# Long convolution with a gated output: the transposed signal's stores on two other queues, two pairs of it loaded early, and whole-partition reads before the last stage

## The chip, the cores and the metric

The kernel runs on one core of a Trainium2 chip. The metric is device time in microseconds from start to end of one execution. Five engines take part: TensorE (PE, its weight loads PEld), VectorE (DVE), ScalarE (ACT), GpSimd (POOL) and SyncE (SP). Each runs its own list of instructions in order and waits for the others by semaphores. A DMA is issued by one engine (it stands in that engine's list and waits its turn there) and is then carried by 16 DMA engines, which all the queues share. Everything is f32.

## The reference

```python
# x, v: [4, 12800, 128]; pos_emb: [12800, 64]
h = np.maximum(pos_emb @ w1, 0) @ w2 * np.exp(-0.01 * pos)[:, None]
y = causal convolution of (x * v) with h along the sequence, per channel (by FFT)
z = x * y
gate = sigmoid(sum over k < 5 of conv_w[k] * z shifted down by 4 - k)   # per channel
out = (gate * (z @ w_val)) @ w_out
```

## The kernel before

The convolution is a transform over a split index: 12800 positions are J = 2 halves of N1 = 100 by N2 = 64. Two arrays in DRAM stand between three stages: `a_u`, the signal after the transform over N1, 105 MB in both directions together, and `c_y`, the product with the filter's spectrum, transformed back over N2, about as much. Instructions are put in each engine's list in the order in which the code issues them.

**Stage 1 (lines L232 to L388, up to some 356 us)** has 64 iterations. For each, `fetch` (L306) loads 1 MB of x and v into one of five `ld` tiles, seven iterations ahead, on SP's queue. `product` (L312, DVE) multiplies them; `mirrored` (every second iteration) makes sums and differences `eo` on DVE (L321) and POOL (L322), in two buffers by turns; `spectra` does 12 matmuls into `fp` (L334, PE) and two evictions into `st` (L336, ACT; four buffers). `store` writes the first 100 partitions of `st` to `a_u`, on SP's queue and one iteration late: each iteration calls `store(*last)`, and `_Split` (L118) makes two DMAs of it, 96 rows and 4 rows. In between, a generator `fil` puts the work on the filter (`gp`, `ap`, `fk`, `ag`) into the lists of PE, DVE and ACT, a portion each iteration. In iteration 62 the table of weights (`in_tab_w`) and 24 of the 32 slices of pair 0 of `a_u` are loaded.

**Stage 2 (L391 to L520, to some 755 us)** goes over 50 pairs p of frequencies. `load_pair` reads 1 MB of `a_u` for a pair (L227; L213 where `load_a` reads a part of one), two pairs ahead. `filter_pair` (L404) makes the pair's filter, evicted into `h_sb` (L409); `spectrum` (L419) transforms the signal into `z_ps`; `times` (L425, DVE) multiplies both into `va`, `vb`, `vc`, `vd`; POOL adds them (L504 to L506); `inverse` transforms back into `c_ps` (L435), ACT copies that into `c_sb` (L442; two tiles, each with both halves j) and stores 512 KB to `c_y` from ACT's queue (L443). From p = 34 on, `load_k` (L202) reads rows of `c_y` that are complete into `ag` blocks, for the first FIRST = 3 steps of stage 3.

**Stage 3 (L530 to L725)** has 32 steps s of R = 4 rows. `load_rows` reads the step's 2 MB of `c_y` into two `ag` blocks, by `_Split` in eight DMAs of 96 or 4 partitions, and `load_x` a tile `xr` (L545), on SP. `y_sum` (L596, PE, with the table `inv`, over 100 partitions) makes `sd`, `y_copy` (L603, ACT) copies it to `sd_sb`, `y_trans` (L610) transposes it, `y_join` (L621 on DVE, L623 on POOL) multiplies by x into `ext`; then come the five taps (L638, DVE), the sigmoid (L644), the two products (`v_ps` L649, `o_ps` L659) and the store of the result from ACT's queue (L671). The tiles of this stage lie in pools opened when stage 2's are closed.

Of the kernel before, what the change touches and what calls it, by code (L numbers as in the profile page):

```python
# [28 lines left out]
R = 4  # L29
WARM = 4  # L30
NC1 = N1 // 2 + 1


def _tables():
# [87 lines left out]
def tile_longconv_gate(  # L122
# [28 lines left out]
    c_y = dram.tile([J, N1, 2 * N2, B, D], F32, name="c_y")  # L151
# [3 lines left out]
    inv = const.tile([N1, 2, N2], F32, name="inv")  # L155
# [19 lines left out]
    nc.scalar.dma_start(out=inv, in_=t_inv)  # L175
# [16 lines left out]
    blocks = [ag.rearrange("p k j e -> p (k j e)")[:N1, i * CR:(i + 1) * CR] for i in range(N1 * J * FO // CR)]  # L192
# [3 lines left out]
    def block(s, c):  # L196
        return blocks[(2 * s + c) % len(blocks)]

    def load_k(s, c, k0, k1):
        j, g = y_order[s]  # L200
        n0 = c * N2 + g * R
        nc.sync.dma_start(  # L202
            out=block(s, c)[k0:k1], in_=c_y[j, k0:k1, n0:n0 + R].rearrange("k p b d -> k (p b d)"))
# [3 lines left out]
    weights, loaded, NL = [], {}, 24  # L207
# [24 lines left out]
    with tc.tile_pool(name="p1", bufs=1) as p1, tc.tile_pool(name="ps1", bufs=1, space=PSUM) as ps1:  # L232
# [106 lines left out]
        def store(q, s, st):  # L339
            sync_s.dma_start(  # L340
                out=a_u[:, s, q].rearrange("k e j b d -> k (e j b d)"),
                in_=st[:N1].rearrange("k e j b d -> k (e j b d)"))

        fetched, us, eos, last = {}, {}, {}, None
        with tc.manual_schedule():
# [15 lines left out]
            for n in range(N2):  # L361
# [26 lines left out]
            store(*last)  # L388


    with tc.tile_pool(name="p2", bufs=1) as p2, tc.tile_pool(name="ps2", bufs=1, space=PSUM) as ps2:  # L391
# [3 lines left out]
        def bank():  # L395
            return ps2.tile([128, BD], F32, name="z_ps", bufs=4)

        def filter_pair(p):

            h_ps = ps2.tile([128, J, BD], F32, name="c_ps", bufs=2)[:, :, 0:2 * D].rearrange("p j (c d) -> p j c d", c=2)  # L400
# [28 lines left out]
        def inverse(p, j, terms):  # L429
            wk = loaded[p][1]  # L430
            c_ps = ps2.tile([128, 2, BD], F32, name="c_ps", bufs=2)
# [6 lines left out]
            if j == 0:  # L438
                c_sb = p2.tile([128, 2, J, B, D], F32, name="c_sb", bufs=2)
                outs[p] = c_sb  # L440
            c_sb = outs[p]
            nc.scalar.copy(out=c_sb[:, :, j].rearrange("p h b d -> p h (b d)"), in_=c_ps)  # L442
            nc.scalar.dma_start(  # L443
                out=c_y[j, 2 * p:2 * p + 2].rearrange("h p b d -> p h (b d)"),
                in_=c_sb[:, :, j].rearrange("p h b d -> p h (b d)"))

        outs = {}
# [11 lines left out]
        with tc.manual_schedule():  # L459
            for p in range(-1, NP + 1):  # L460
                now, nxt, old = 0 <= p < NP, p + 1 < NP, 0 <= p - 1
                if p < 0:
                    load_a(loaded[0][0], 0, NL, N2 // 2)
                for q in range(AHEAD + 1) if p < 0 else (p + AHEAD,):
                    if q < NP and q not in loaded:
                        loaded[q] = load_pair(q)
                if p in early:
                    load_k(*early.pop(p))
# [26 lines left out]
                if now:  # L495
                    vc = p2.tile([128, 2, B, D], F32, name="vc", bufs=3)
                    vd = p2.tile([128, 2, B, D], F32, name="vd", bufs=2)
                    times(vc, z1[0], h[:, 0, 0:2], 2)
# [5 lines left out]
                    nc.gpsimd.tensor_tensor(va[:, 0:2], va[:, 0:2], vb[:, 0:2], op=ALU.add)  # L504
                    nc.gpsimd.tensor_tensor(vcf, vcf, vdf, op=ALU.add)  # L505
# [4 lines left out]
                if old:  # L510
                    if p < NP:
                        inverse(p - 1, 0, ((0, oa[:, 0]), (1, oa[:, 1])))
                    if p == NP - 1:
                        inverse(p, 0, ((0, va[:, 0]), (1, va[:, 1])))
                        for c in range(2):
                            load_k(0, c, 96, N1)
                    inverse(p - 1, 1, ((0, oa[:, 2]), (1, oa[:, 3, 0:PB]), (0, oc[:, 0]), (1, oc[:, 1])))
            for s in range(1, FIRST):
                for c in range(2):
                    load_k(s, c, 80, N1)  # L520
# [9 lines left out]
    with tc.tile_pool(name="p3", bufs=1) as p3, tc.tile_pool(name="ps3", bufs=1, space=PSUM) as ps3:  # L530
# [8 lines left out]
        def load_x(s):  # L539
# [4 lines left out]
            xr = p3.tile([D, R * ROW], F32, name="xr", bufs=2)  # L544
# [47 lines left out]
        def y_sum(s, r):  # L592
            ct, _ = loads3[s]
            sd = ps3.tile([128, B * D], F32, name="sd", bufs=2)
            for c in range(2):
                nc.tensor.matmul(  # L596
                    out=sd[c * N2:(c + 1) * N2], lhsT=inv[:, c], rhs=ct[c][:, r * B * D:(r + 1) * B * D],
# [3 lines left out]
        def y_copy(s, r):  # L601
            t = p3.tile([128, B, D], F32, name="sd_sb", bufs=3)
# [3 lines left out]
        def y_trans(s, r):  # L606
            t = sds.pop((s, r))
            tp = ps3.tile([D, B, 128], F32, name="tp3", bufs=2)
            for b in range(B):
                nc.tensor.transpose(out=tp[:, b], in_=t[:, b], identity=ident)  # L610
            dif = p3.tile([D, B, NC1], F32, name="dif", bufs=3)
# [3 lines left out]
        def y_join(s, r):  # L615
# [3 lines left out]
            yr = p3.tile([D, B, N1], F32, name="yr", bufs=2)  # L619
# [59 lines left out]
        with tc.manual_schedule():  # L679
# [93 lines left out]
```

## Time and profile before

| | |
|---|---|
| median of 3 runs | 1147.57 us (1146.57 to 1148.95) |
| the profiled execution | 1147.54 us |
| its span, from the first to the last instruction | 1145.8 us |
| granted TensorE clock, mean | 0.970 |
| busy: PE, DVE, POOL, ACT | 1041.9, 969.1, 781.2, 615.9 us |
| moved by DMA | 344.60 MB, 301 GB/s over the span |

The page of the profile gives each engine's busy time over the whole span. The stages have different limits, so busy times in stretches of a stage, the waits in it and the chain of the work that ended last say more. A rate in GB/s counts what the DMA engines moved in a stretch, and the DMA share is the mean part of it in which they were busy.

### The profile page before, as it was taken

The numbers are of one execution on the slowest core, as the hardware profiler recorded it, in microseconds if no ns is written. First come the engines' busy times: TensorE is split into PE (matmuls) and PEld (weight loads), VectorE is DVE, ScalarE is ACT, GpSimd is POOL, SyncE is SP. The second block draws the span as 40 slices with busy tenths as digits, with TensorE's granted clock in tenths as the row PEclk, the third lists the DMA queues.
The fourth block names the chain that finished last, engine by engine and source line by source line (L and its number), as shares of the span: only waits on it lengthen the run. The fifth ranks groups of instructions, "written<-read, shape, count | busy, mean of one in ns | idle before, by whom it ended". The sixth has DMA issues, their size and how long they took to land.

```text
span 1145.8 us, 17528 instructions
## 1 busy us (share of the span) xinstructions
PE 1041.9 (91%) x6208; PEld 490.5 (43%) x6208; DVE 969.1 (85%) x1150; ACT 615.9 (54%) x1003; POOL 781.2 (68%) x393
## 2 busy tenths in 40 slices
PE   4899898777874999999999999988999999999996
PEld 2455554433431344444444444433444444444442
DVE  5675545799844999999999999819999999999997
ACT  1366555766751344444344434337777767767674
POOL 3353432233312888988898888928999899999981
PEclk9999998999995899999999999989999999999999
DMA  9999999999987688888888999575999999999952
GB/s 361 367 413 406 366 361 358 345 358 345 361 265 291 223 307 310 299 309 304 307 285 284 364 352 329 192 212 165 297 283 297 277 296 291 293 292 287 291 174 115
DMA packets 93176, 344.60 MB, mean 301 GB/s; under 512 B 9806, under 2 KB 19706, under 8 KB 77898
## 3 DMA queue, kind: packets, MB, share of 16 engines
q1 hardware_dynamic: 58824, 263.74, 70.2%
q10 hardware_dynamic: 34266, 79.74, 18.1%
q8 instruction: 51, 0.84, 0.3%
q14 instruction: 35, 0.29, 0.1%
HBM read 212.37 MB, written 131.07 MB: 300 GB/s over the span
## 4 chain that ended last, share of the span: by engine, by line
PE 66%; DMA 24%; DVE 5%; ACT 3%; issue 1%; SPq 0%; ACTq 0%; DVEq 0%
PE c_ps L435 22%; DMA a_u<-st 13%; PE sd L596 10%; PE z_ps L419 9%; DMA ld<-in_xv_dram 8%; PE o_ps L659 7%; PE v_ps L649 6%; PE tp L610 5%; PE fp L334 3%; PE c_ps L404 2%; DMA ld<-in_pos_dram 2%; DVE gt L638 1%; DVE fk L284 1%; ACT st L336 1%; PE gp L292 1%
## 5 line engine op out<-in xcount | busy, mean ns | idle before, releaser
L623 POOL TENSOR_TENSOR ext<-yr,xr 128x400 f32<-128x400 f32 x120 | 304.6, 2540 | 34.3 <-DVE yr L621 31.3
L322 POOL TENSOR_TENSOR eo<-eo 128x512 f32<-128x512 f32 x62 | 120.0, 1954 | 204.6 <-DVE eo L321 204.6
L638 DVE SCALAR_TENSOR_TENSOR gt<-ext,cw,gt 128x1600 f32<-128x1600 f32 x128 | 241.1, 1884 | 2.4 <-ACT gt L635 2.4
L334 PE MATMUL fp<-eo,fold 64*128 64x512 f32 x768 | 196.3, 646 | 51.1 <-ACT st L336 36.5
L442 ACT COPY c_sb<-c_ps 128x1024 f32<-128x1024 f32 x100 | 101.3, 1013 | 203.2 <-PE c_ps L435 193.9
L336 ACT COPY st<-fp 128x1024 f32<-128x1024 f32 x128 | 124.5, 1015 | 130.0 <-DMA a_u<-st 71.4
L435 PE MATMUL c_ps<-va,ld 64*128 64x512 f32 (+1 forms) x800 | 165.3, 552 | 0.0
L425 DVE TENSOR_TENSOR va<-z_ps,h_sb 128x2048 f32<-128x2048 f32 x50 | 114.4, 2287 | 36.9 <-DMA ld<-a_u 30.0
L504 POOL TENSOR_TENSOR va<-va,vb 128x1024 f32<-128x1024 f32 x50 | 118.4, 2367 | 39.9 <-DVE vb L425 39.9
L419 PE MATMUL z_ps<-ld 64*64 64x512 f32 x800 | 122.7, 620 | 17.2 <-DMA ld<-a_u 15.7
L334 PEld LDWEIGHTS fp<-eo,fold 64*128 64x128 f32 x768 | 75.0, 198 | 133.6 <-issue 76.4
L596 PE MATMUL sd<-ag,inv 100*64 100x512 f32 x512 | 129.1, 622 | 0.2 <-DMA ag<-c_y 0.2
L435 PEld LDWEIGHTS c_ps<-va,ld 64*128 64x128 f32 x800 | 73.7, 188 | 112.8 <-issue 110.0
L659 PE MATMUL o_ps<-gd,wout 128*128 128x400 f32 x256 | 111.5, 517 | 10.7 <-DVE gd L654 8.7
L506 POOL TENSOR_TENSOR va<-va,vb 128x1024 f32<-128x1024 f32 x50 | 118.2, 2363 | 0.0
L425 DVE TENSOR_TENSOR vb<-z_ps,h_sb 128x2048 f32<-128x2048 f32 x50 | 114.0, 2281 | 0.0
L603 ACT COPY sd_sb<-sd 128x512 f32<-128x512 f32 x128 | 76.6, 599 | 64.2 <-PE sd L596 55.8
L649 PE MATMUL v_ps<-ext,wval 128*128 128x400 f32 x256 | 107.2, 500 | 0.0
L610 PEld LDWEIGHTS tp<-ident,sd_sb 128*128 128x128 f32 x512 | 59.4, 143 | 81.4 <-PE sd L596 49.6
L435 PE MATMUL c_ps<-vc,ld 64*128 64x512 f32 x400 | 94.2, 589 | 0.0
L505 POOL TENSOR_TENSOR vc<-vc,vd 128x768 f32<-128x768 f32 x50 | 91.1, 1822 | 2.2 <-issue 0.3
L610 PE MATMUL tp<-ident,sd_sb 128*128 128x128 f32 x512 | 81.3, 284 | 7.0 <-ACT sd_sb L603 5.7
(84 smaller groups left out, 1452.7 us busy)
## 6 DMA issues: line engine op xcount, KB each, us to landing
ld<-in_xv_dram SPq DMA_DIRECT2D x64, 1024.0 KB
c_y<-c_sb ACTq DMA_DIRECT2D x100, 512.0 KB
ld<-a_u SPq DMA_DIRECT2D x49, 1024.0 KB
a_u<-st SPq DMA_DIRECT2D x64, 768.0 KB
ag<-c_y SPq DMA_DIRECT2D x116, 384.0 KB
xr<-in_xt_dram SPq DMA_DIRECT2D x31, 800.0 KB
out_dram<-o_sb ACTq DMA_DIRECT2D x31, 800.0 KB
ld<-in_tab_w_dram SPq DMA_DIRECT2D x12, 768.0 KB
```

Source lines behind the costliest of these rows:

```text
L322: eng.tensor_tensor(eo[:, s, :, 0], eo[:, s, :, 0], eo[:, s, :, 1], op=ALU.subtract)
L334: nc.tensor.matmul(out=fp[:, h], lhsT=fold[r, w], rhs=eo[r, o, :, l], start=i == 0, stop=i == len(terms) - 1)
L336: nc.scalar.copy(out=st[:, o].rearrange("k j (h b) d -> k h j (b d)", h=2), in_=fp)
L419: nc.tensor.matmul(out=zs[c][half[h]], lhsT=wk[half[c], 0, half[h]], rhs=a2[half[c], h, j], start=True, stop=True)
L425: nc.vector.tensor_tensor(out, z.rearrange("p (b d) -> p b d", d=D).unsqueeze(1).to_broadcast([128, n, B, D]), h_sb.unsqueeze(2).to_broadc ...
L435: nc.tensor.matmul(out=c_ps[:, h, 0:n], lhsT=wk[half[h], 1 + c], rhs=vt[half[h]].rearrange("p b d -> p (b d)"), start=(i == 0), stop=(i == ...
L596: nc.tensor.matmul(out=sd[c * N2:(c + 1) * N2], lhsT=inv[:, c], rhs=ct[c][:, r * B * D:(r + 1) * B * D], start=True, stop=True)
L610: nc.tensor.transpose(out=tp[:, b], in_=t[:, b], identity=ident)
L623: nc.gpsimd.tensor_tensor(e[:, r0 + r], yr, xr, op=ALU.mult)
L638: nc.vector.scalar_tensor_tensor(gt, rows(t, k), cw[:, k:k + 1], gt, op0=ALU.mult, op1=ALU.add)
L649: nc.tensor.matmul(out=v_ps, lhsT=wval, rhs=rows(t)[:, r * ROW:(r + 1) * ROW], start=True, stop=True)
L659: nc.tensor.matmul(out=o_ps, lhsT=wout, rhs=gd, start=True, stop=True)
```

## The change

Stage 1 stores each iteration's `st` in that iteration: 96 rows from ACT's queue, behind the two evictions that fill it, and 4 rows from POOL's. SP's queue keeps the loads alone. In iteration 60 the weights and 28 of the 32 slices of pairs 0 and 1 are loaded; the other 4 of each follow when stage 1's stores are issued.

In stage 2 each `c_sb` eviction has a tile of its own (five buffers). Of the last pair's three additions two go to DVE. All last rows of `c_y` for steps 0 to 2 are asked for within pair 49, none behind it. The table `inv` is loaded at p = 4 into the tile of the `fold` table, which is no longer needed then, and not at the start.

In stage 3 the tiles of the chain from `sd` to `yr` and `xr` are in pools of their own, which are opened first, in place of tiles that share room with stage 2's. `c_y` is laid out with both halves j below one another, 200 rows, and a block is read by one DMA of 128 rows, 1 MB: rows 0 to 127 for j = 0, rows 72 to 199 for j = 1. `inv` has zeros for the 28 rows that do not belong to j, and `y_sum` runs over 128 partitions. Two warming matmuls instead of four stand ahead of the stage.

```diff
-        def store(q, s, st):
-            sync_s.dma_start(
-                out=a_u[:, s, q].rearrange("k e j b d -> k (e j b d)"), in_=st[:N1]...)
+            for eng, r in ((nc.scalar, slice(0, 96)), (nc.gpsimd, slice(96, N1))):
+                eng.dma_start(
+                    out=a_u[r, s, q].rearrange("k e j b d -> k (e j b d)"), in_=st[r]...)
...
-                if n == N2 - 2:
-                    loaded[0] = load_pair(0, NL)              # NL = 24
-                if last:
-                    store(*last)
-                last = q, s, st
+                if n == N2 - 4:
+                    for p in range(2):
+                        loaded[p] = load_pair(p, NL)          # NL = 28
+                store(q, s, st)
...
-            store(*last)
+            for p in range(2):
+                load_a(loaded[p][0], p, NL, N2 // 2)
...
-            if j == 0:
-                c_sb = p2.tile([128, 2, J, B, D], F32, name="c_sb", bufs=2)
+            c_sb = p2.tile([128, 2, BD], F32, name="c_sb", bufs=5)
...
+                    if not nxt:
+                        nc.vector.tensor_tensor(va[:, 0:2], va[:, 0:2], vb[:, 0:2], op=ALU.add)
...
-                rows_ = c_y[j].rearrange("k p b d -> k p (b d)")
-                for h in range(0, R, R // 2):
-                    sync_s.dma_start(
-                        out=t[:, h * B * D:(h + R // 2) * B * D],
-                        in_=rows_[:, n0 + h:n0 + h + R // 2].rearrange("k p e -> k (p e)"))
+                nc.sync.dma_start(
+                    out=t, in_=c_y[j * EDGE:j * EDGE + 128, n0:n0 + R].rearrange("k p b d -> k (p b d)"))
...
+            k = slice(0, N1 if s < NG else 128)
...
-                    out=sd[c * N2:(c + 1) * N2], lhsT=inv[:, c], rhs=ct[c][:, r * B * D:(r + 1) * B * D],
+                    out=sd[c * N2:(c + 1) * N2], lhsT=inv[k, s // NG, c], rhs=ct[c][k, r * B * D:(r + 1) * B * D],
...
-    with tc.tile_pool(name="p3", bufs=1) as p3, tc.tile_pool(name="ps3", bufs=1, space=PSUM) as ps3:
+    with tc.tile_pool(name="y3", bufs=1) as y3, tc.tile_pool(name="psy", bufs=1, space=PSUM) as psy, \
+            tc.tile_pool(name="p3", bufs=1) as p3, tc.tile_pool(name="ps3", bufs=1, space=PSUM) as ps3:
```

Line numbers after the change are some two higher (L306 is L308, L334 is L336, L336 is L338). SP's list at the end of stage 1, behind the last load of x and v, before (`ld<-in_tab_w` is the table of weights, `ld<-a_u` a part of pair 0, which in the list below of the change is a part of pair 0 or 1; the stores are those of the last four iterations):

```order
L118 DMA a_u<-st 96x2048
L118 DMA a_u<-st 4x2048
L221 DMA ld<-in_tab_w_dram 128x4x384
L213 DMA ld<-a_u 48x2x1024 x2
L118 DMA a_u<-st 96x2048
L118 DMA a_u<-st 4x2048
L118 DMA a_u<-st 96x2048
L118 DMA a_u<-st 4x2048
L213 DMA ld<-a_u 16x2x1024
L118 DMA a_u<-st 96x2048
L118 DMA a_u<-st 4x2048
L213 DMA ld<-a_u 16x2x1024
```

The same place in SP's list now:

```order
L308 DMA ld<-in_xv_dram 128x2048 x50
L223 DMA ld<-in_tab_w_dram 128x4x384
L215 DMA ld<-a_u 56x2x1024 x4
L215 DMA ld<-a_u 8x2x1024 x4
L229 DMA ld<-a_u 128x2x1024 x2
```

The stores have left SP's list; the large parts of two pairs and then the small ones stand behind the last load. ACT's list in the last iterations of stage 1, where the last portion of the filter's work ends, before:

```order
L281 ACTIVATE fk<-dft,tw 128x128 x4
L295 COPY ag<-gp 128x512
L336 COPY st<-fp 128x2x2x256 x2
L295 COPY ag<-gp 128x512
L336 COPY st<-fp 128x2x2x256 x12
```

and now, with a store behind each iteration's two evictions and that iteration's portion of the filter:

```order
L283 ACTIVATE fk<-dft,tw 128x128 x4
L297 COPY ag<-gp 128x512
L343 DMA a_u<-st 96x2048
L338 COPY st<-fp 128x2x2x256 x2
L297 COPY ag<-gp 128x512
L343 DMA a_u<-st 96x2048
L338 COPY st<-fp 128x2x2x256 x2
L343 DMA a_u<-st 96x2048
```

POOL's list there had the subtractions alone; now each pair of subtractions (for the next q) has the 4-row stores of two iterations behind it:

```order
L324 TENSOR_TENSOR eo_109<-eo_109 128x2x256 x2
L343 DMA a_u<-st 4x2048 x2
L324 TENSOR_TENSOR eo_108<-eo_108 128x2x256 x2
L343 DMA a_u<-st 4x2048 x6
L506 TENSOR_TENSOR va<-va,vb 128x1024
```

A subtraction now stands behind stores that wait for evictions. SP's list from the last reads of `c_y` in stage 2 to the first full block of stage 3, before:

```order
L202 DMA ag<-c_y 16x2048 x2
L202 DMA ag<-c_y 4x2048 x2
L202 DMA ag<-c_y 20x2048 x4
L545 DMA xr<-in_xt_dram 128x1600 x2
L118 DMA ag<-c_y 96x1024
L118 DMA ag<-c_y 4x1024
```

and now:

```order
L204 DMA ag<-c_y 16x2048 x6
L204 DMA ag<-c_y 4x2048 x6
L549 DMA xr<-in_xt_dram 128x1600 x2
L561 DMA ag<-c_y 128x2048 x2
L549 DMA xr<-in_xt_dram 128x1600
```

Eight DMAs of a step have become two.

More of the change, by code (lines that the diff above doesn't have):

```diff
@@ L149, in tile_longconv_gate @@
     a_u = dram.tile([N1, 2, N2 // 2, 2, J, B, D], F32, name="a_u")
-    c_y = dram.tile([J, N1, 2 * N2, B, D], F32, name="c_y")
+    c_y = dram.tile([J * N1, 2 * N2, B, D], F32, name="c_y")
     fwd = const.tile([N1, 3, N1], F32, name="fwd")
     fold = const.tile([128, 3, 128], F32, name="fold")
-    inv = const.tile([N1, 2, N2], F32, name="inv")
+    inv = fold[:, 0:2].rearrange("p j (c n) -> p j c n", c=2)
     win = const.tile([N1, J, N2], F32, name="win")
@@ L202, in load_k @@
         nc.sync.dma_start(
-            out=block(s, c)[k0:k1], in_=c_y[j, k0:k1, n0:n0 + R].rearrange("k p b d -> k (p b d)"))
+            out=block(s, c)[k0:k1], in_=c_y[j * N1 + k0:j * N1 + k1, n0:n0 + R].rearrange("k p b d -> k (p b d)"))
     NP, PG = N1 // 2, KG // 2
-    weights, loaded, NL = [], {}, 24
+    weights, loaded, NL = [], {}, 28
     def load_a(a2, p, n0, n1):
@@ L395, in bank @@
         def bank():
-            return ps2.tile([128, BD], F32, name="z_ps", bufs=4)
+            return psz.tile([128, BD], F32, name="z_ps", bufs=4)
         def filter_pair(p):
-            h_ps = ps2.tile([128, J, BD], F32, name="c_ps", bufs=2)[:, :, 0:2 * D].rearrange("p j (c d) -> p j c d", c=2)
+            h_ps = psc.tile([128, J, BD], F32, name="c_ps", bufs=2)[:, :, 0:2 * D].rearrange("p j (c d) -> p j c d", c=2)
             for c in range(2):
@@ L430, in inverse @@
             wk = loaded[p][1]
-            c_ps = ps2.tile([128, 2, BD], F32, name="c_ps", bufs=2)
+            c_ps = psc.tile([128, 2, BD], F32, name="c_ps", bufs=2)
             for i, (c, vt) in enumerate(terms):
@@ L437, in inverse @@
                         start=(i == 0), stop=(i == len(terms) - 1))
-            if j == 0:
-                c_sb = p2.tile([128, 2, J, B, D], F32, name="c_sb", bufs=2)
[L440 to L447, printed above, removed]
+            c_sb = p2.tile([128, 2, BD], F32, name="c_sb", bufs=5)
+            nc.scalar.copy(out=c_sb, in_=c_ps)
+            nc.scalar.dma_start(out=c_y[j * N1 + 2 * p:j * N1 + 2 * p + 2].rearrange("h p b d -> p h (b d)"), in_=c_sb)
         filt_p, z_p, v_p = {}, {}, {}
@@ L466, in tile_longconv_gate @@
                         loaded[q] = load_pair(q)
+                if p == 4:
+                    nc.sync.dma_start(out=inv, in_=t_inv)
                 if p in early:
@@ L601, in y_copy @@
         def y_copy(s, r):
-            t = p3.tile([128, B, D], F32, name="sd_sb", bufs=3)
+            t = y3.tile([128, B, D], F32, name="sd_sb", bufs=3)
             nc.scalar.copy(out=t.rearrange("p b d -> p (b d)"), in_=sds.pop((s, r)))
@@ L684, in tile_longconv_gate @@
             for _ in range(WARM):
-                w_ps = ps3.tile([D, 2 * D], F32, name="o_ps", bufs=2)
-                nc.tensor.matmul(
-                    out=w_ps, lhsT=ident, rhs=dft.rearrange("p a k -> p (a k)"), start=True, stop=True)
+                w_ps = psy.tile([D, B, 128], F32, name="tp3", bufs=2)
+                nc.tensor.matmul(out=w_ps[:, 0:2], lhsT=ident, rhs=dft, start=True, stop=True)
             for i in range(R * NT + AHEAD3 + R + 3):
@@ L694, in tile_longconv_gate @@
                     if g == NG - 1:
-                        tails[j] = p3.tile([D, R, B, N1], F32, name="tail", bufs=2)
+                        tails[j] = y3.tile([D, R, B, N1], F32, name="tail", bufs=2)
                     elif g % EG == 0:
```

54 lines of the change are left out of this document (28 added, 26 removed).

## The prediction

> **What bounds the kernel now.** I read the page first, its chain by line above all, then busy times in stretches of each stage, and last the two seams between the stages.
>
> ```profile
> PE c_ps L435 22%; DMA a_u<-st 13%; PE sd L596 10%; PE z_ps L419 9%; DMA ld<-in_xv_dram 8%; PE o_ps L659 7%; PE v_ps L649 6%; PE tp L610 5%; PE fp L334 3%; PE c_ps L404 2%; DMA ld<-in_pos_dram 2%; DVE gt L638 1%; DVE fk L284 1%; ACT st L336 1%; PE gp L292 1%
> ```
>
> The chain runs through DMAs where stage 1 is (`a_u<-st`, `ld<-in_xv_dram`: 21% of the span), and through matmuls in the other two. Stretches inside the stages say the same (columns: the stretch, its length, busy us of PE, PEld, DVE, ACT, POOL with instructions, granted clock, DMA share, GB/s):
>
> ```profile
> 49.00:99.00 50.00, 47.04 (x408) 27.48 (x408) 36.70 (x30) 29.73 (x34) 24.38 (x11) 1.00 1.01 411
> 120.00:180.00 60.00, 52.32 (x526) 30.29 (x524) 26.59 (x25) 31.59 (x39) 21.15 (x11) 0.97 0.99 362
> 180.00:320.00 140.00, 111.58 (x512) 56.78 (x514) 118.01 (x189) 91.94 (x175) 44.82 (x26) 0.95 0.99 354
> 376.00:735.00 359.00, 359.00 (x2618) 157.56 (x2616) 352.04 (x330) 147.54 (x232) 320.71 (x189) 1.00 0.86 302
> 790.00:1106.00 316.00, 314.36 (x1336) 145.37 (x1336) 314.43 (x446) 229.70 (x399) 286.43 (x113) 1.00 0.96 285
> ```
>
> The first three rows are stage 1. No engine is full, the DMA engines always are, and yet they move 411 GB/s in one stretch and 354 to 362 in the others, with the same two large transfers per iteration. The fourth is stage 2: PE is busy for all of it. The fifth is stage 3: PE and DVE have 1.6 us of slack in 316. So the room is in stage 1's transfers and at the seams. The waits of 60 to 342 us name it (who waits for what: us in all, times, longest):
>
> ```profile
> ACT st L336 <- DMA a_u<-st: 71.4, 36, 3.8
> PEld fp L334 <- ACT st L336: 34.5, 42, 3.2
> DVE ld L312 <- DMA ld<-in_xv_dram: 33.1, 10, 4.9
> ```
>
> ACT waits for an `st` buffer whose store hasn't landed, and PE behind it for ACT: the late stores hold up the chain more than the loads do.
>
> **Stage 1, the stores.** Removed from SP are 64 issues of 96 rows and 64 of 4, which stood one iteration late behind a load (the order of time: start, us, engine and line; then two groups: busy us, mean ns):
>
> ```profile
> 200.51 0.35 SPq L306 DMA_DIRECT2D ld<-in_xv_dram  x1
> 200.96 2.36 SPq L118 DMA_DIRECT2D a_u<-st  x2
> 742.87 0.37 ACTq L443 DMA_DIRECT2D c_y<-c_sb  x1
> L322 POOL TENSOR_TENSOR eo<-eo 128x512 f32<-128x512 f32 x62 | 120.0, 1954 | 204.6 <-DVE eo L321 204.6
> L321 DVE TENSOR_TENSOR eo<-u,ld 128x1024 f32<-128x1024 f32 x64 | 76.5, 1236 | 4.0
> ```
>
> SP spends 0.35 us on a load and 2.36 us (waits included) on two stores, during which no further load goes out. Now loads wait on SP for their buffer only, and stores go out behind their own eviction. With more transfers outstanding, the engines should starve less. The bound above: 120 to 320 us moves 60 x 362 + 140 x 354 = 71.3 MB, which at the 411 GB/s of the first stretch takes 173 us, 27 less. DVE, with 118.0 busy in 140, would still fit in 140 x 354 / 411 = 121, and PE's 52.3 of 60 in 60 x 362 / 411 = 53. The bound below: in stage 2, where ACT's stores already mix with SP's loads, the engines move 302 / 0.86 = 351 GB/s while busy; at that rate 71.3 MB takes 203 us, 3 more. The first row is nearer in kind, the second in queues, so I take the middle, **-12 us**, and keep -27 and +3.
>
> The cost on the issuing engines is hidden. On ACT, 64 issues of 0.37 us are 24 us over the stage; an iteration moves 1.05 MB in and 0.82 out, 5.3 us at 354 GB/s, so 180 to 320 us hold 26 and their issues 10 us, where ACT is busy 91.9 of 140: 38 to spare. On POOL no DMA issue is in the trace: between the 0.37 us of ACT's and the 1.95 of POOL's own operation, 64 of them cost 24 to 125 us of a stage in which POOL is busy 44.8 of 140; I take 1 us each. More matters what stands behind: both subtractions for the next q now wait until the evictions of this q are done (about 2 us after its last matmul, two of 1.01) and the issue is through. Their result is there 2 + 1 + 2 x 1.95 = 6.9 us after that matmul, and is due two iterations after it: 10.6 us, or 9.1 at 411 GB/s. Free; it stays so up to 3.2 us an issue.
>
> A rule speaks against this term. The Trainium skill ("DMA: Bandwidth & Descriptors", section "Issuing engines are not separate DMA queues") says that DMAs issued from several engines still run on the same 16 DMA engines, so spreading them buys issue time and no bandwidth. The DMA share of 0.99 agrees with it; the 411 beside 354 GB/s at that same share says that a full share isn't a full rate. By that rule the term is 0 and the sum 12 us higher.
>
> **Seam 1 to 2.** The seam in the order of time, its chain (start, us, what), and its busy times:
>
> ```profile
> 335.71 0.57 SPq L221 DMA_DIRECT2D ld<-in_tab_w_dram  x1
> 340.28 1.01 ACT L336 COPY st<-fp 128x1024 f32<-128x1024 f32 x1 [0.72 <-PE fp L334]
> 360.32 2.29 DVE L425 TENSOR_TENSOR va<-z_ps,h_sb 128x2048 f32<-128x2048 f32 x1 [29.97 <-DMA ld<-a_u]
> ```
>
> ```profile
> 340.08 10.31 DMA a_u<-st
> 350.82 4.43 DMA a_u<-st
> 355.63 4.70 DMA ld<-a_u
> ```
>
> ```profile
> 341.00:360.00 19.00, 2.97 (x43) 1.83 (x47) 0.00 (x0) 2.48 (x7) 0.00 (x0) 0.61 0.71 228
> ```
>
> The last eviction ends at 341.29; the first product of stage 2 starts at 360.32. In these 19.0 us the engines do next to nothing (PE 2.97): a store of 10.31 us (queued behind weights and half of pair 0 on the one queue), the last of 4.43 issued only then, and a read of 4.70. With the stores behind their evictions and the weights and both pairs' large parts ahead, only the last store and small reads remain: 0.1 + 4.43 + 0.35 + 4.70 = 9.6. That is **-9 us**. If the store of the iteration before it is still in the queue, 5 of that are lost (-4); if the last store takes 1.9 (its 0.79 MB at the 418 GB/s of reads, below), it is -12. The work that this brings forward (pair 1) is 1 MB that stage 2 has to read anyway with the engines 0.86 busy.
>
> **Stage 2.** PE is busy for 359.00 of 359.00 us; nothing the change does there (c_sb tiles, one 0.1 MB table read at p = 4) touches PE. **0**. At the start the table is no longer loaded: 0.05 MB, 0.1 us of a stretch that transfers fill; **0**.
>
> **Seam 2 to 3.**
>
> ```profile
> 739.32 2.36 POOL L504 TENSOR_TENSOR va<-va,vb 128x1024 f32<-128x1024 f32 x1
> 745.56 1.01 ACT L442 COPY c_sb<-c_ps 128x1024 f32<-128x1024 f32 x1 [2.72 <-DMA c_y<-c_sb]
> 753.26 1.04 PE L596 MATMUL sd<-ag,inv 100*64 100x512 f32 x2 [0.16 <-DMA ag<-c_y]
> 759.44 1.07 ACT L603 COPY sd_sb<-sd 128x512 f32<-128x512 f32 x2 [8.39 <-DMA c_y<-c_sb]
> ```
>
> `sd` is there at 754.3, but its copy waits until 759.44 for the store out of the room that `sd_sb` shares with `c_sb`; and a `c_sb` eviction waited 2.72 us for a store. With own tiles both waits go: 759.44 - 754.3 = 5.1 and up to 2.7, and the last pair's first addition takes DVE 1.24 instead of POOL 2.36, 1.1 less. All together 8.9; late next are the reads of the last rows, on which `sd` itself waits (0.16 now), so I take **-8 us**. If the reads are what comes last, -5 stays; -11 if the `xr` load, which starts at about the same time, was late as well. Two warming matmuls less stand in the wait for those reads; if the clock rose later for it, PE would show it here, where it is granted 0.50 already (762 to 764 us, below): 0.
>
> **Stage 3, the reads.** With PE and DVE full, a step keeps its length unless the reads become the bound. Stretches filled by one kind of transfer, and two issues of `xr`:
>
> ```profile
> 342.00:343.00 1.00, 0.45 (x19) 0.21 (x8) 0.00 (x0) 0.00 (x0) 0.00 (x0) 1.00 1.01 223
> 358.00:362.00 4.00, 3.87 (x25) 2.04 (x29) 1.68 (x1) 0.20 (x1) 0.00 (x0) 0.50 1.02 418
> 710.00:711.50 1.50, 1.50 (x26) 0.60 (x16) 1.50 (x3) 1.01 (x2) 1.46 (x2) 1.00 0.89 199
> 762.00:764.00 2.00, 2.00 (x8) 0.47 (x4) 0.23 (x1) 0.58 (x1) 1.03 (x1) 0.50 1.02 419
> 865.00:870.00 5.00, 5.00 (x24) 2.48 (x22) 5.00 (x9) 4.42 (x8) 4.59 (x3) 1.00 1.01 263
> ```
>
> ```profile
> 872.02 0.35 SPq L545 DMA_DIRECT2D xr<-in_xt_dram  x1
> 883.31 0.35 SPq L545 DMA_DIRECT2D xr<-in_xt_dram  x1
> ```
>
> In order: a 48-partition read of `a_u` 223 GB/s, a 128-partition one 418, an 80-row read of `c_y` 199, `xr` (128 partitions) 419, `c_y` by 96 and 4 rows 263. The step is 883.31 - 872.02 = 11.29. Now 1.64 MB of `c_y` take 6.2 us at 263 GB/s; 128 rows are 2.10 MB, at 418 GB/s 5.0 us, with `xr` and the result at 0.82 MB and some 2.0 us each 9.0 of 11.29. The matmul over 128 partitions has as many columns as the one over 100: same price. **0**.
>
> **The sum.** -12 - 9 - 8 = -29 against the profiled execution of 1147.54 us, which lies 0.03 under the median: **1118.5 us**. By the ends of the terms it is 1097.5 (-27, -12, -11) to 1141.5 (+3, -4, -5); not all fall to one side, so I give the forecast's own range as 1104 to 1130.
>
> **Rivals.**
>
> *A: the spread of queues gives no rate.* The DMA share is 0.99 already, and stage 2's mixed queues move only 351 GB/s. Then stage 1 keeps its length, and the seams remain: 1147.5 - 17 = 1130.5.
>
> *B, the slower side: the 128-row read of `c_y` stays as slow per byte as the others.* All slow rows but one are reads of `c_y`, so its layout in DRAM (rows of the partitions 256 KB apart) may be the reason, not the number of partitions. At 263 GB/s the step's 2.10 MB take 8.0 us, with 2.0 + 2.0 it is 12.0; at 199 it is 14.5. The step is then 0.7 to 3.2 us longer, times 29 steps +20 to +93; with -29 that gives 1138 to 1212, and about 1160 at 240 GB/s between the two (12.8 us a step). It decides from 2.10 / (11.29 - 4.0) = 288 GB/s down, and makes the whole slower than before from 253 down (1.0 us a step). Against it: `a_u` read over 48 partitions is as slow (223), over 128 fast. The Trainium skill ("SBUF — State Buffer", section "Door 1: The DMA port swizzle") says that a tile on half of the partitions reaches 8 of the 16 ports and one on all 128 reaches all; the 223 beside 418 GB/s for the same array agrees.
>
> *C: the issuing engines hold stage 1 up.* POOL's stores delay `eo`, or ACT's issues wait in front of evictions for a completion of an earlier transfer. Against it the slack above, for it that PE already waits 34.5 us for ACT. It decides once POOL's issue is over 3.2 us, or ACT's waits over the 38 spare us. With stage 1's 12 gone, as in A, and 0.15 us lost in each of 64 iterations: about 1140.
>
> *D: stage 1 moves 411 GB/s all through:* -27 there, 1103.5, the end of the forecast's own case.
>
> **How the numbers follow.** The forecast, with D as its low end, has 0.49, A 0.25, C 0.13, B 0.13, most of it slower. A and the forecast lie below 1131; C from 1131 to 1150; B above 1138. To leave out no more than 2 in 10 (B's slow part and the outer ends), the range is 1102 to 1142. A difference of 0.2% (2.3 us) is what a measurement here can tell from none. Faster: the forecast, A, most of C and the least of B, 0.84; same: 0.04, from C and B; slower: 0.12, B and the tail of C.
>
> **What would show it.** In the changed profile: 120 to 300 us at 380 GB/s or more, and the last eviction of stage 1 near 329 (A: 341); from there to the first product of stage 2 about 10 us; no wait of `sd_sb` for a store of `c_y`; in stage 3 stretches of reads at some 415 GB/s and `xr` issued every 11.29 us (B: 12 or more, with DVE no longer full). In stage 1 the wait of ACT for `a_u` should fall well below 71 us; C would show as PE waiting for POOL's `eo`. The prediction is wrong above all if the DMA engines in stage 1 keep 354 GB/s, or if the 128 rows don't read at the rate of `xr`.

## The result and the profile after

The changed kernel takes 1137.57 us (median of 10 runs, 1132.36 to 1143.12), the kernel before 1147.07 (10 runs, 1141.02 to 1151.17): a ratio of 0.991 (0.989 to 0.994). That is 9.5 us less; 29 were forecast. The measured time lies inside the range of 1102 to 1142, close to its slow end, and the gain is a third of the forecast.

The profiled execution of the changed kernel took 1132.36 us, 5 below the median; a second profile of it took 1145.28. So one profile of this kernel says little by itself, and below several are set side by side. The page after, its span and chain by line:

```profile
span 1130.1 us, 17247 instructions
PE 64%; DMA 20%; DVE 11%; issue 3%; ACT 3%; SPq 0%; ACTq 0%; DVEq 0%
PE c_ps L439 20%; DMA ld<-in_xv_dram 15%; PE sd L598 10%; PE z_ps L423 9%; PE o_ps L661 7%; PE v_ps L651 6%; PE tp L612 5%; DMA ld<-in_pos_dram 3%; PE fp L336 3%; PE c_ps L408 2%; DVE gt L640 2%; DVE fk L286 2%; DMA a_u<-st 1%; DVE va L429 1%; DVE vb L429 1%
```

`a_u<-st` has nearly left the chain (13% before, 1% now), and the loads have taken its place (15%, 8% before): in stage 1 the chain still runs through transfers. The stretches that were shown of before, here in the first profile after (stage 3 to 1080 us; columns as in the prediction):

```profile
49.00:99.00 50.00, 45.39 (x364) 26.57 (x364) 35.16 (x29) 28.06 (x32) 26.54 (x22) 0.93 0.98 375
120.00:180.00 60.00, 54.69 (x560) 32.02 (x556) 33.70 (x29) 37.00 (x45) 27.87 (x25) 0.98 1.01 404
180.00:320.00 140.00, 113.85 (x522) 57.07 (x520) 125.73 (x194) 92.59 (x174) 63.08 (x56) 0.94 0.97 362
376.00:735.00 359.00, 356.32 (x2592) 157.03 (x2590) 350.21 (x330) 147.47 (x230) 318.33 (x186) 1.00 0.86 300
790.00:1080.00 290.00, 289.01 (x1228) 133.84 (x1226) 288.43 (x410) 212.95 (x369) 263.44 (x103) 1.00 0.85 332
```

and stage 1 in the second:

```profile
120.00:180.00 60.00, 52.93 (x524) 29.58 (x520) 28.48 (x23) 33.43 (x38) 23.27 (x21) 0.94 0.95 347
180.00:320.00 140.00, 112.73 (x514) 57.91 (x516) 123.05 (x193) 92.13 (x174) 61.60 (x55) 0.93 0.97 358
```

The same program moved 404 GB/s in one execution and 347 in the other in 120 to 180 us; the kernel before moved 362. The forecast wanted 380 or more through the whole stage. Stage 3 is as full as before, at a DMA share of 0.85 instead of 0.96.

Four times tell a profile apart: the end of the last eviction of stage 1; from there to the first product of stage 2 (`va`, DVE); from the first to the last `va` (373.5 to 375.8 us in every profile here); from the last `va` to the end of the span.

| profile | last eviction at | seam 1 to 2 | last `va` to end | ratio to before, interval |
|---|---|---|---|---|
| before | 341.3 | 19.0 | 411.9 | 1 |
| the change | 334.3 | 12.3 | 409.8 | 0.991 (0.989 to 0.994) |
| after_again | 346.4 | 13.6 | 409.0 | 0.992 (0.989 to 0.995) |
| stores_only | 335.8 | 10.2 | 411.8 | 0.989 (0.986 to 0.991) |
| early_only | 354.6 | 12.4 | 412.0 | 1.002 (1.000 to 1.005) |
| stage23_only | 342.0 | 18.0 | 408.9 | 0.996 (0.994 to 0.999) |
| warm_off | 339.2 | 11.6 | 412.7 | 0.988 (0.985 to 0.992) |
| reads96 | 341.3 | 13.0 | 409.7 | 0.989 (0.985 to 0.993) |
| after_half | 308.2 | 14.0 | 409.5 | 0.960 (0.956 to 0.964) |
| after_nofk | 338.1 | 10.3 | 409.2 | 0.986 (0.983 to 0.989) |
| before_half | 304.0 | 18.1 | 410.1 | 0.962 (0.960 to 0.965) |
| best1 | 340.5 | 9.9 | 408.9 | 0.988 (0.986 to 0.991) |
| best2 | 344.8 | 9.9 | 407.4 | 0.989 (0.984 to 0.993) |
| after_pad | 344.8 | 13.0 | 410.7 | 0.993 (0.990 to 0.996) |
| before_pad | 348.0 | 18.3 | 410.4 | 0.999 (0.996 to 1.002) |
| after_112 | 324.9 | 10.9 | 408.7 | 0.976 (0.973 to 0.979) |
| before_112 | 318.3 | 18.7 | 410.4 | 0.979 (0.976 to 0.983) |
| best3 | 333.9 | 9.7 | 406.6 | 0.975 (0.971 to 0.979) |

Stage 1's end carries the scatter. With the stores of before it lies at 341.3, 342.0 and 348.0 us (before, stage23_only, before_pad), with those of the change at 334.3, 346.4, 339.2, 341.3 and 344.8 (the change, after_again, warm_off, reads96, after_pad): means of 343.8 and 341.2. Some of these profiles are of executions 5 us or so away from their kernel's median, so 2.6 us between two such means says little. The seams scatter less: 18.0 to 19.0 us in the first group, 11.6 to 13.6 in the second.

### The profile page after: what moved, and what is told of

It reads as the page before. It is cut to its first block, busy times and chain, and to the rows that moved or that the text cites. A ratio compares the mean times of both kernels' runs of the same rounds, so it can differ in the third digit from the quotient of the medians.

```text
span 1130.1 us, 17247 instructions
## 1 busy us (share of the span) xinstructions
PE 1038.0 (92%) x6204; PEld 490.2 (43%) x6204; DVE 977.8 (87%) x1152; ACT 619.5 (55%) x1003; POOL 803.6 (71%) x455
## 4 chain that ended last, share of the span: by engine, by line
PE 64%; DMA 20%; DVE 11%; issue 3%; ACT 3%; SPq 0%; ACTq 0%; DVEq 0%
PE c_ps L439 20%; DMA ld<-in_xv_dram 15%; PE sd L598 10%; PE z_ps L423 9%; PE o_ps L661 7%; PE v_ps L651 6%; PE tp L612 5%; DMA ld<-in_pos_dram 3%; PE fp L336 3%; PE c_ps L408 2%; DVE gt L640 2%; DVE fk L286 2%; DMA a_u<-st 1%; DVE va L429 1%; DVE vb L429 1%
## 5 line engine op out<-in xcount | busy, mean ns | idle before, releaser
L336 PE MATMUL fp<-eo,fold 64*128 64x512 f32 x768 | 193.7, 640 | 30.2 <-ACT st L338 15.9
L324 POOL TENSOR_TENSOR eo<-eo 128x512 f32<-128x512 f32 x62 | 113.0, 1840 | 103.3 <-DVE eo L323 103.2
L338 ACT COPY st<-fp 128x1024 f32<-128x1024 f32 x128 | 126.2, 1016 | 105.5 <-PE fp L336 75.8
L423 PE MATMUL z_ps<-ld 64*64 64x512 f32 x800 | 122.7, 620 | 10.3 <-issue 8.9
L598 PE MATMUL sd<-ag,fold 100*64 100x512 f32 (+1 forms) x512 | 127.8, 615 | 3.3 <-DMA ag<-c_y 3.3
L336 PEld LDWEIGHTS fp<-eo,fold 64*128 64x128 f32 x768 | 73.3, 198 | 111.9 <-issue 66.3
L343 POOL DMA_DIRECT2D a_u<-st x64 | 34.0, 533 | 85.7 <-ACT st L338 85.6
```

The source lines that it names most:

```text
L336: nc.tensor.matmul(out=fp[:, h], lhsT=fold[r, w], rhs=eo[r, o, :, l], start=i == 0, stop=i == len(terms) - 1)
L338: nc.scalar.copy(out=st[:, o].rearrange("k j (h b) d -> k h j (b d)", h=2), in_=fp)
L423: nc.tensor.matmul(out=zs[c][half[h]], lhsT=wk[half[c], 0, half[h]], rhs=a2[half[c], h, j], start=True, stop=True)
L598: nc.tensor.matmul(out=sd[c * N2:(c + 1) * N2], lhsT=inv[k, s // NG, c], rhs=ct[c][k, r * B * D:(r + 1) * B * D], start=True, stop=True)
```

## The experiments

**The parts alone.** One run repeats the changed kernel; one gives the kernel before the new stores and nothing else; one gives it the early loads alone; one is the changed kernel with stage 1 of before.

```diff
 stores_only (from before)
-            sync_s.dma_start(out=a_u[:, s, q]..., in_=st[:N1]...)          # and: one iteration late
+            for eng, r in ((nc.scalar, slice(0, 96)), (nc.gpsimd, slice(96, N1))): ...
 early_only (from before)
-                if n == N2 - 2: loaded[0] = load_pair(0, NL)               # NL = 24
+                if n == N2 - 4: for p in range(2): loaded[p] = load_pair(p, NL)   # NL = 28
```

> The changed kernel once more, with a second profile and its own comparison on one chip. Theory E (stage 1 is bound by its engines once the stores are out of the way): the last eviction ends again near 334 us, DVE is 0.85 to 0.95 busy in 180 to 300 us, and the comparison gives about 8 to 12 us less than before. Theory T (the transfers still bound it, and their rate varies from run to run): the last eviction moves by some us between the two profiles, with the GB/s of 180 to 300 us.

> The kernel before with the stores alone moved (96 rows on ACT's queue, 4 on POOL's, same iteration). If the stores carry the gain of stage 1 and of the seam behind it: last eviction near 334 us instead of 341, the first product of stage 2 some 10 to 13 us earlier, 10 to 13 us less in all. If the early loads carry the seam: 7 us less.

> The kernel before with the early loads alone (weights and 28 of 32 slices of pairs 0 and 1 asked for in iteration 60, on SP's queue ahead of the last stores). If the place of the stores is what matters at the seam, two pairs more in front of them make it longer: 0 to 5 us more than before. If the early loads carry the seam's gain: 4 to 7 us less.

> The changed kernel with stage 1 of the kernel before (stores on SP, one iteration late, one pair loaded early). Prediction's theory: the seam 2 to 3 gives 8 us less. Rival: two warming matmuls, which now stand in PE's list ahead of the last inverse transforms and wait there for VectorE, take some 3.5 us of that back: 2 to 4 us less than before.

The stores alone give 13 us, no less than the whole change, but 8.8 of them are the shorter seam (19.0 to 10.2) and not stage 1. The early loads alone give nothing (their shorter seam is paid by a later last eviction, 354.6). Stages 2 and 3 alone give 4, less than the 8 of the prediction and as much as its rival had. Between the two profiles of the changed kernel, 12 us of stage 1's end go with the GB/s: theory T.

**Is stage 1 bound by transfers or by its engines?** Half of the loads' bytes; and nearly none of the `fk` work of ACT and DVE.

```diff
 after_half, before_half
-  dma_start(out=t, in_=xv[...])               ; tensor_tensor(u, t[:, 0], t[:, 1], op=ALU.mult)
+  dma_start(out=t[:, 0:1024], in_=xv[...][:, 0:1024]) ; tensor_tensor(u, t[:, 0], t[:, 0], op=ALU.mult)
 after_nofk
+                if k0 < 8:                     # ahead of the activations and products that make fk
```

> The changed kernel, loading x alone in stage 1 and squaring it: half of the bytes of the loads (0.52 of 1.87 MB per iteration less), all instructions of the engines the same; v is left out. Theory T (transfers bound stage 1 also after the change): the last eviction comes 30 us or more earlier than 334 to 346 us, up to where DVE is full, and the time falls as much. Theory E (its engines bound it): less than 10 us.

> The changed kernel with the table fk of the filter made for the first 8 frequencies only and reused: 92 of 100 activations and as many DVE operations of 180 to 320 us are left out. Theory T: stage 1 keeps its end (334 to 346 us) and the time stays within 4 us of the changed kernel's. Theory E: 10 to 20 us less.

> The kernel before, loading x alone in stage 1 and squaring it (v is left out). If the place of the stores matters apart from the rate (ACT waiting for st buffers): the last eviction comes later than in the changed kernel with half loads (308 us), at 315 to 325. If the transfers' rate alone matters: 305 to 310 as there, and the time 9 to 10 us more than its 1104 (the seams).

With half of the loads the last eviction comes at 308.2 us, and at 304.0 with the stores of before: the place of the stores is worth nothing in stage 1 when the transfers have room (DMA share 0.89 and 0.80 in 180 to 300 us). The two times are near each other as well (0.960 and 0.962 of before, where 9 to 10 us between them were expected): the longer seam of before_half is made up by its earlier last eviction. Without `fk` the last eviction stays at 338.1 (by its ratio, 0.986 beside 0.991 and 0.992, some 5 us may be the engines'). Transfers bound the stage, before and after.

**Transfers by themselves.** No arithmetic; the first kernel does loads, then stores as 96 and 4 rows, then both in turns on one queue. Its stretches (length, busy DVE and POOL, clock, share, GB/s):

> Transfers alone, no arithmetic and no result: 24 loads of 1.05 MB on SP, then 24 stores of 0.82 MB (96 and 4 rows) on ACT, then 24 of both in turns on SP, then 24 of both with loads on SP, 96 rows on ACT and 4 on POOL. Theory M (reads and writes at the same time cost rate, by themselves): about 415 GB/s in the first two stretches, 350 to 380 in the third and fourth. Rival (the engines' traffic or waits of stage 1 cost it): 405 or more in all four.

```profile
25.00:60.00 35.00, 0.00 (x0) 0.00 (x0) 1.00 1.01 421
75.00:115.00 40.00, 0.00 (x0) 0.00 (x0) 1.00 0.89 288
150.00:230.00 80.00, 0.00 (x0) 0.00 (x0) 1.00 0.99 377
```

Neither theory: the loads run at 421, the stores alone at 288, slower than the mixture. 1.05 MB at 421 and 0.82 at 288 are 2.5 + 2.8 = 5.3 us an iteration, 350 GB/s, which is what stage 1 does. (In turns the two moved 377. The fourth stretch, with the 4 rows from POOL, ran unevenly, between 197 and 429 GB/s from one 10 us to the next, and isn't read further.) So the stores themselves came under suspicion, and the second kernel varies their form. Its stretches stand in the order of its expectation: 96 and 4 rows at 512 KiB, at 516 KiB; 128 rows at 512, at 516, connected; 96 rows without the 4, in turns with loads.

> Stores alone, from ACT's queue, no arithmetic and no result. In turn 20 stores each of: 96 and 4 rows at a row pitch of 512 KiB (as a_u has it); the same at 516 KiB; 128 rows at 512 KiB; 128 rows at 516 KiB; 128 rows of one connected megabyte; then 24 stores of 96 rows at 516 KiB in turns with loads. Theory P (rows a power of two apart in DRAM slow the stores): about 285 GB/s at 512 KiB, 400 or more at 516 KiB and connected, whatever the rows. Theory R (96 and 4 of 128 partitions slow them): 285 in the first two stretches, 400 or more in the next three. If stores as such are slow: 285 to 330 in all five.

```profile
20.00:60.00 40.00, 0.00 (x0) 0.00 (x0) 1.00 0.90 288
70.00:110.00 40.00, 0.00 (x0) 0.00 (x0) 1.00 0.92 300
130.00:160.00 30.00, 0.00 (x0) 0.00 (x0) 1.00 1.01 421
170.00:200.00 30.00, 0.00 (x0) 0.00 (x0) 1.00 1.01 419
210.00:240.00 30.00, 0.00 (x0) 0.00 (x0) 1.00 1.01 420
290.00:370.00 80.00, 0.00 (x0) 0.00 (x0) 1.00 1.01 423
```

The pitch does next to nothing, and 96 partitions are no slower than 128. (They were run in turns with loads only; the same mixture with the 4 rows moved 377 in the first kernel.) What the slow stretches have and the last has not is the transfer over 4 partitions. In the two slow ones the 8 KB packets took 312 ns at the median, over 350 ns in 37 to 38 of 100 and over 600 ns in 14 to 15; in the stretches of 128 rows none took over 350 ns.

The count of packets says something of the reason. A 128-row store has 16 packets of 4 bytes beside its 128 of 8 KB (193 to 1540 in the third stretch); a pair of 96 and 4 rows has 20 beside its 100 (277 to 1407 in the first). This suggests, and doesn't prove, that 4 of the 16 DMA engines carry the 4 rows. They would then get seven rows where the others get six, and the engines' mean share in stores alone could be 6.25 / 7 = 0.89 at most, by this estimate; 0.89 to 0.92 was measured. That alone would leave 376 of 421 GB/s. The rest of the loss is the stretched packets, and no run separates what stretches them.

The pitch in the whole kernels, 4 KiB of room behind each row of `a_u`:

```diff
-    a_u = dram.tile([N1, 2, N2 // 2, 2, J, B, D], F32, name="a_u")
+    a_u = dram.tile([N1, 2 * N2 * J * B * D + 1024], F32, name="a_u")[:, 0:2 * N2 * J * B * D].rearrange(...)
```

> The changed kernel with 4 KiB of room behind each row of a_u (pitch 516 instead of 512 KiB), nothing else; the order on every engine is the same. Theory P: stage 1 moves about 400 GB/s throughout, the last eviction ends at 315 to 325 us instead of 334 to 346, and the time is 15 to 20 us less than the changed kernel's. Otherwise within 4 us of it.

> The kernel before with the same room in a_u. Theory P: stage 1 is 15 us or more shorter here too, and stores on SP, one iteration late, take no more for it than stores on ACT's queue: the difference to the changed kernel with room is that of the seams, 8 to 10 us. If the room does nothing: within 4 us of the kernel before.

Ratios of 0.993 and 0.999: nothing, as the transfers alone had it.

**The store in one piece.** 112 partitions are 16 times 7; the 12 rows more are never read.

```diff
-    a_u = dram.tile([N1, 2, N2 // 2, 2, J, B, D], F32, name="a_u")
+    a_u = dram.tile([112, 2, N2 // 2, 2, J, B, D], F32, name="a_u")
...
+            nc.scalar.dma_start(out=a_u[:, s, q]..., in_=st[0:112]...)    # after_112; nc.sync and late in before_112
```

> The changed kernel with one store of 112 partitions on ACT's queue in place of 96 rows there and 4 on POOL's (a_u has 12 more rows, which nobody reads): 0.92 MB instead of 0.82, one transfer instead of two. Theory F (the transfer over 4 partitions slows its neighbours): 400 GB/s or more in 99 to 300 us, the last eviction at 305 to 320 us, near the 308 of half loads, and 15 to 28 us less than the changed kernel. Rival (loads and stores at once cost the rate, whatever their form): 350 to 380 GB/s, and with 5% more bytes 10 to 15 us more.

> The kernel before with one store of 112 partitions in place of 96 and 4 rows, still on SP's queue and one iteration late. Theory F: 400 GB/s or more here too, the last eviction at 310 to 325 us instead of 341, 15 to 25 us less than before; then the queue of the stores was not what held stage 1. Rival (the store's place holds it as well): less than half of the gain that the changed kernel has from this.

Stage 1 in before, in before_112 and in after_112:

```profile
99.00:180.00 81.00, 72.62 (x741) 42.24 (x737) 38.66 (x33) 44.83 (x55) 29.50 (x16) 0.98 0.99 370
180.00:300.00 120.00, 95.09 (x432) 48.19 (x434) 100.16 (x167) 78.62 (x151) 37.90 (x22) 0.94 0.98 352
```

```profile
99.00:180.00 81.00, 77.67 (x775) 44.65 (x772) 44.62 (x42) 52.41 (x69) 33.79 (x18) 1.00 1.01 425
180.00:300.00 120.00, 100.78 (x474) 51.98 (x476) 111.32 (x179) 85.17 (x161) 42.17 (x25) 0.96 1.01 415
```

```profile
99.00:180.00 81.00, 72.31 (x740) 42.56 (x740) 43.68 (x36) 48.08 (x58) 27.11 (x16) 0.95 1.01 410
180.00:300.00 120.00, 104.68 (x494) 54.27 (x490) 114.79 (x182) 88.67 (x168) 43.51 (x25) 0.95 1.01 413
```

At a DMA share of 0.98 or more in all of them the rate goes from 352 to 415 and 413. Of the 8 KB packets in 180 to 240 us, 7.3% took over 600 ns in before, 0.4% in before_112. The old store order, on SP and one iteration late, with this one edit has its last eviction at 318.3 us and is 24 us faster than before: more than twice what the whole change brought. In after_112 the last eviction comes at 324.9, later than theory F had it, and the total is what it had. The form of the store held stage 1, and the queue did not.

**The seam 2 to 3, the early loads, the reads.**

```diff
 warm_off: WARM = 0        reads96: eight reads of 96 and 4 rows per step, y_sum over 100 partitions
 best1: the change without the early loads (24 of 32 slices of pair 0 in iteration 62, as before)
 best2 (from best1)
-                    for s in range(FIRST):
-                        for c in range(2):
-                            load_k(s, c, 80, 96)                  # steps 1 and 2 now at the end, as before
+                    for c in range(2):
+                        load_k(0, c, 80, 96)
-                w_ps = psy.tile([D, B, 128], F32, name="tp3", bufs=2)
+                w_ps = ps3.tile([D, 2 * D], F32, name="o_ps", bufs=2)   # WARM = 4
 best3: best2 with the 112-row store on ACT's queue
```

> The changed kernel without the two warming matmuls. They stand in PE's list ahead of the inverse transforms of the last two pairs and wait there for VectorE's last product, because their PSUM tiles lie where stage 2's z_ps lay. If this wait takes back part of the seam's gain: the last c_ps matmul ends some 16 us after the last va product instead of 19.6, and the whole takes 3 to 3.5 us less than the changed kernel (about 13 less than the kernel before). Rival: the last reads of c_y are what sd waits for, and they come no earlier: 0 to 1 us less.

> The changed kernel with the eight reads of 96 and 4 rows per step as before, matmuls over 100 partitions. If the reads are hidden behind PE and DVE either way: the step stays at 11.29 us, the DMA share of stage 3 goes from 0.85 back to about 0.96, and the time is that of the changed kernel within 1 us. If the whole-partition reads carry part of the seam or of stage 3: 2 to 3 us more than the changed kernel.

> The changed kernel without the early loads of two pairs: 24 slices of pair 0 in iteration 62 and the other 8 at the start of stage 2, as before. The parts alone gave 0.9887 (stores) and 0.9964 (stages 2 and 3), together 0.9851; the whole change gave 0.991 to 0.992. Theory L (the early loads cost: they share the DMA engines with the last stores): ratio 0.985 to 0.987, the gap from the last eviction to the first product 10 us instead of 12.3 to 13.6. Rival (they cost nothing, the parts do not add up for another reason): ratio near 0.990, gap 12 to 14 us.

> As the kernel without early loads, and the seam 2 to 3 mended: the last rows of step 0 are read first (16 and 4 rows of two blocks, then 20 rows of four), as before, and four warming matmuls stand behind the last inverse transform. Theory S (of the seam's 8 us, the order of these reads takes about 2 to 3 us, the low granted clock after PE's idle time the rest): first transpose about 21 to 22 us after the last va product instead of 25 to 27, first v_ps at 45 to 47 instead of 48 to 50, 3 to 4 us less than without the mending. Rival (the stores of the last pair bound it): within 1 us.

> The changed kernel with the 112-row store, without the early loads of two pairs, and with the seam 2 to 3 mended (rows of step 0 read first, four warming matmuls behind the last inverse transform). By the parts: 15 to 28 us from the store, 2 to 4 from the early loads, about 1.5 from the seam, in all 1105 to 1120 us. If theory F fails: about 1145.

The seam in the changed kernel, in the order of time:

```profile
729.17 1.10 PE L688 MATMUL tp<-dft,ident 128*128 128x256 f32 x4 [2.68 <-DVE vd L429]
739.96 1.01 ACT L443 COPY c_sb<-c_ps 128x1024 f32<-128x1024 f32 x1 [1.99 <-PE c_ps L439]
742.94 1.04 PE L598 MATMUL sd<-ag,fold 100*64 100x512 f32 x2 [3.02 <-DMA ag<-c_y]
745.86 0.59 ACT L605 COPY sd_sb<-sd 128x512 f32<-128x512 f32 x1 [4.88 <-PE sd L598]
```

The 8.39 us of `sd_sb` behind a store are gone, but `sd` itself now starts 22.6 us after the last `va` (720.35), where it started 19.3 us after it (733.92 to 753.26): the reads of step 0's last rows stand behind the 16-row reads of steps 1 and 2. And the warming matmuls now stand ahead of the last inverse transforms and wait 2.68 us for DVE. Taking them out frees those transforms (they end 15.6 us after the last `va` instead of 19.6), but `sd`, which waits for the reads, starts only 1.0 us earlier (21.6 after the last `va`), as the rival of that run had it. PE idles longer before it, and the granted clock is low for longer behind it. The end part in this profile is 2.9 us longer than the changed kernel's (412.7 to 409.8); by the ratios, 0.988 and 0.991, the two totals aren't told apart. PE in warm_off, and in the changed kernel (columns as in the prediction's stretches):

```profile
740.00:746.00 6.00, 0.08 (x2) 0.00 (x0) 0.00 (x0) 1.01 (x1) 0.00 (x0) 0.68 0.64 184
746.00:757.00 11.00, 10.94 (x27) 4.28 (x28) 0.65 (x3) 2.46 (x6) 1.03 (x1) 0.50 0.95 210
```

```profile
744.00:748.00 4.00, 3.73 (x9) 1.20 (x10) 0.00 (x0) 1.02 (x2) 0.00 (x0) 0.59 0.96 84
748.00:757.00 9.00, 9.00 (x51) 4.20 (x49) 3.19 (x10) 4.60 (x13) 5.08 (x5) 0.99 0.99 396
```

After 6 us of idleness PE ran 11 us at 0.50. With the reads in the old order and the warming matmuls last (best2) `sd` starts 19.7 us after the last `va`, and the end part is 407.4 us, 1.5 less than in best1, half of what theory S gave; its total isn't told apart from best1's. Without the early loads the seam 1 to 2 is 9.9 us in best1 instead of 10.3 to 14.0 in the kernels that have them and the old stores' size; by the ratios that cost isn't resolved (0.988 for best1, 0.991 and 0.992 for the change, and the intervals overlap). The reads by 96 and 4 rows cost nothing in stage 3 (share 0.97 at 289 GB/s, PE and DVE full): they are hidden either way. best3 is the fastest version tried, 1119.46 us against 1149.34 before, though its difference to after_112 (1121.16) lies inside the intervals.

## Why the prediction was wrong, point by point

- **Stage 1, -12: this step failed.** The means of the table give -2.6, within the scatter. The step read "with more transfers outstanding, the engines should starve less" out of 354 beside 411 GB/s at a full share. They did not starve. The DMA engines were held up by the pair of transfers of 96 and 4 rows, and the change kept that pair; "the same two large transfers per iteration" passes over the small third one. One store of 112 rows in place of the pair gave 24 us with the queue of before. Rival A had stage 1 right; its time, 1130.5, is 7 below the measured 1137.6, because it took both seams at their full price. The Trainium skill ("DMA: Bandwidth & Descriptors", section "Issuing engines are not separate DMA queues") says what rival A says: DMAs issued from several engines run on the same 16 DMA engines, and only time on the issuing engines is saved. The means of 343.8 and 341.2 agree with it. What the first stretch of 411 GB/s showed was right in one respect only: the transfers could run at that rate. There 1.2% of the 8 KB packets took over 600 ns, in 120 to 180 us 6.1%; why so few in the first stretch stays open.
- **ACT's wait of 71.4 us for `a_u`** was read as a sign of late stores. It was a symptom of the rate. In the changed kernel no wait of `st` in 60 to 342 us is put down to `a_u<-st` any more, in either profile, as the prediction wanted, and yet the stage is no shorter beyond the scatter. With 112 rows on SP, still late, the wait is 45.2 us in 60 to 320 us (65.8 before in the same stretch), and the stage is 23 us shorter:

```profile
ACT st L336 <- DMA a_u<-st: 45.2, 32, 2.7
```

- **Seam 1 to 2, -9: right in kind, -6 in size.** It takes 12.3 to 13.6 us instead of 9.6. In the changed kernel the last store was issued at 334.32 and held ACT up until 341.57, 7.25 us, and the one before it took 7.62 in the chain; the sum had 4.43 for the last. The early loads of two pairs run beside them. Without these the seam is 9.9 (best1) and 10.2 (stores_only), close to the sum. That the early loads are the reason is likely and not fully shown, since after_nofk has them and a seam of 10.3. The last store and the wait for it, the chain after, and the chain in stores_only:

```profile
334.32 0.31 ACTq L343 DMA_DIRECT2D a_u<-st  x1
341.57 0.59 ACT L413 COPY h_sb<-c_ps 128x512 f32<-128x512 f32 x1 [7.28 <-DMA a_u<-st]
```

```profile
331.22 7.62 DMA a_u<-st
338.84 5.53 issue
```

```profile
332.75 5.82 DMA a_u<-st
338.65 3.23 DMA ld<-a_u
```

- **Stage 2, 0: right** (373.6 and 373.8 us from first to last `va`).
- **Seam 2 to 3, -8: this term was mis-sized; it measured -2 to -3** (end part 411.9 before; 409.8, 409.0 and, in stage23_only, 408.9). Both waits went, as forecast. "Late next are the reads" was priced from a wait of 0.16 us that held in the old order of reads; the new order, which stood in the lists, makes it 3.02. The prediction kept -5 for the case that the reads come last, and that was too much as well. The warming matmuls' place in PE's list was overlooked, and their effect was called 0.
- **Stage 3, 0: right, and rival B did not come about.** Two reads of 128 rows need a DMA share of 0.85, and `xr` is issued every 11.29 us. A stretch filled by them and a little of `xr` moved 429 GB/s; in reads96, with the new layout of `c_y` and the old form of reads, a stretch moved 243. So the layout was not what made the reads slow. The issues of `xr` in the changed kernel, then the stretch in the changed kernel and the one in reads96:

```profile
788.17 0.33 SPq L549 DMA_DIRECT2D xr<-in_xt_dram  x1
799.46 0.33 SPq L549 DMA_DIRECT2D xr<-in_xt_dram  x1
```

```profile
859.00:864.00 5.00, 5.00 (x24) 2.33 (x22) 5.00 (x7) 4.67 (x8) 4.79 (x2) 1.00 1.02 429
870.00:875.00 5.00, 5.00 (x22) 2.48 (x22) 5.00 (x8) 3.46 (x7) 4.59 (x3) 1.00 1.05 243
```

  The argument against B, that fewer than 128 partitions are what is slow, is no rule: stores of 96 rows in turns with loads ran at 423 GB/s, and stage 1 with stores of 112 rows at 410 to 425. The old reads come in pairs of 96 and 4 rows too, as the stores do, and their packets of 4 KB took 249 ns on average in the stretch shown of before, where those of the 128-partition read of `a_u` (358 to 362 us) took 160. No run takes the 4 rows away from the reads alone, so for reads this stays a likeness.
- **Rival C: small.** Its sign, PE waiting for POOL's `eo`, hardly grew: 14.1 us up to 345 us before, 14.4 and 19.1 in the two profiles after. POOL's issue takes 0.53 us, where 1 was taken:

```profile
L343 POOL DMA_DIRECT2D a_u<-st x64 | 34.0, 533 | 85.7 <-ACT st L338 85.6
```

## What to carry to other kernels

A full DMA share beside a rate under the best stretch's, with packets of the same size, means that packets take longer, not that more should be outstanding: look at the forms of the transfers before moving them to other queues. A remainder of a few partitions (100 as 96 and 4) was cheaper here made larger than split off: 12% more bytes in one transfer over 112 partitions took 24 us out of 1149. When a wait is removed, read from the new order what stands ahead of the operation that waited.

## What the runs showed of the hardware

- A transfer over 4 partitions (32 KB) after each one over 96 brings stores from 420 GB/s (128 rows) to 288 and 300, though it has 4% of the bytes. Of the packets that took over 600 ns, half took 672 or more, about two times 309. Stage 1 agrees, in 180 to 300 us: 6.9% of the 8 KB packets took over 600 ns before and 4.2% in the changed kernel, at 352 and 372 GB/s; with 112 rows 1.1% and 1.3%, at 415 and 413.
- In the changed kernel the 4-row stores have a queue of their own. In 180 to 300 us their 8 KB packets took 515 ns on average, those of the loads 343 and those of the 96-row stores 331: all three are slowed, the small transfers most. The Trainium skill ("SBUF — State Buffer", section "Door 1: The DMA port swizzle") says that partitions 96 to 99 lie on one port. No run here measured ports, so whether the slow packets are those that meet there stays open.
- The same program moves 347 or 404 GB/s in 120 to 180 us in different executions, and the packets over 600 ns go with it: 6.3% and 1.9%. The three kernels with stores in one piece moved 396 to 425 in 99 to 300 us, one execution each, so whether they scatter less isn't shown.
- Not settled: why before_112's last eviction is 7 us earlier than that of after_112. That best3's is 9 us later may be scatter: its profiled execution, 1126.35 us, was the slowest of its six.
